# A cached-attention decode kernel: the last V loads in halves released one by one, the keys of pairs 14 and 15 moved up in the load order, and wo in ten pieces

## Chip, cores and metric

One Trainium2 chip; the kernel runs on one of its cores. The metric is device time in microseconds (us). In the profile the engines are PE (TensorE matmuls), PEld (TensorE weight loads), DVE (VectorE), ACT (ScalarE), POOL (GpSimd) and SP (SyncE, which here only issues loads; SPq is its queue). L383 is line 383 of the kernel.

## What is computed

One token goes through a layer norm, then through attention over a cache of 8192 positions in 32 heads, and beside it through a gated unit whose result scales the attention's result. All is float32. Cut to what matters:

```python
xn = layernorm(x)                               # x: 1 x 1 x 512
q  = (xn @ wq)                                  # wq: 512 x 4096, 32 heads of 128
p  = softmax(q . k_cache / sqrt(128))           # k_cache: 32 x 8192 x 128
s  = (p . v_cache) @ wo                         # v_cache the same, wo: 4096 x 512
g  = silu((sigmoid(xn @ w_gate) * (xn @ w_up)) @ w_down)   # 512 x 1376, 1376 x 512
out = x + s * g
```

The two caches are 134.2 MB each, the weights together 25.2 MB; each byte is read once.

## The kernel before, in words

**Tiles.** The 32 heads are taken as NP = 16 pairs. One head of a pair lies on partitions 0 to 63, the other on 64 to 127; each partition holds NB = 128 positions ("columns" below) of 128 numbers, so the keys of a pair, K(i), and its values, V(i), are 8.39 MB each, 64 KB a partition. Three buffers of that size, `slots`, hold them: K of even pairs in slot 1, K of odd pairs in slot 0, every V in slot 2. Pairs are counted from 0, so the last two are 14 and 15.

**One pair.** `scores(i)` (L377) on DVE multiplies the whole of K(i) by the query in place (L383) and sums each position's 128 products (L384), then takes a maximum (L386). PE turns the maximum and spreads it, DVE reduces it (L375, `all_max`), ACT takes the exponentials (L398, `powers_of`) into `weights`. PE then multiplies these by V(i) in 32 matmuls of four columns each (L356, each in two records of the trace, so 64), adding up in `po`. ACT copies `po` (L405), PE gathers the diagonal blocks (L361), DVE places them (L391, `heads_out`). On DVE the order is scores of pair i first, then `heads_out` of pair i - 1, then `all_max` of pair i.

PE's program is noted first and played later: `pair` is one body of a loop over the 16 pairs, so that a wait or count which it contains is there in every pair. All PE instructions therefore carry L37 in the trace. `taken(sem, n)` waits on a semaphore and takes n off it.

**Loads.** All big loads go through SP's one queue in program order, each of them split over the 16 DMA engines. Where an issue has to wait (for a buffer to come free), every load behind it in the program waits too. `summed[i]` counts the end of pair i's scores on DVE and frees its K buffer; `valued` counts pairs whose V matmuls are done and frees slot 2. In the main loop at L408, round i issues K(i) once `summed[i - 2]` is there, then V(i - 1) once `valued` is i - 1. In the last round K(15) and V(14) and V(15) are each cut at column 84 of 128, and the order is K(15) first part, both parts of V(14), K(15) second part, both parts of V(15).

**Output projection.** After V(15), six pieces of wo are issued into slot 1, ending at rows `W_ENDS` = 14, 24, 28, 30, 31, 32 of the 32 rows that a partition holds. Rows below `W_DVE` = 16 are multiplied and added on DVE in two sums, `part` (L466, L468, joined in L472); rows 16 to 29 are matmuls into `big[0]`; `to_fold` adds the two on DVE (L448), and `fold` brings the sum into `acc` by matmuls. Rows 30 and 31 (from `W_FOLD`) go straight into `acc`. Two DVE operations (L497, L499) apply the gate and add x, and SP stores the 2 KB result (L512).

**The start.** Layer norm, the queries and the gated unit run ahead of the loop, while wq, w_gate, w_up and K(0) are loaded; the issues are at the top, ahead of the body.

Of the kernel before, what the change touches and what calls it, by code (L numbers as in the profile page):

```python
# [14 lines left out]
EPS = 1e-5  # L15
# [35 lines left out]
def kernel(  # L51
# [18 lines left out]
    NB = S // HP  # L70
    NP = H // 2
    NG = 4
    GP = P // NG
    GC = D // NG
    QT = 512
    HT = QT // Dh
# [10 lines left out]
    FC = FL // GP  # L87
    assert F <= 3 * QT and FL % GP == 0 and 2 * KT * F <= SLOT and (FP + FC) * D <= SLOT // 2

    W_ENDS, W_DVE, W_FOLD = (14, 24, 28, 30, 31, 32), 16, 30  # L90
    V_CUT, K_CUT = 84, 84

    DVE, ACT, SP, POOL = nc.vector, nc.scalar, nc.sync, nc.gpsimd
    PE = Later(nc.tensor)
# [9 lines left out]
    def sb(name, *shape):  # L104
        return nc.alloc_sbuf_tensor(name, [P, *shape], F32)[:]
# [6 lines left out]
    st, eps_t = sb("st", 16), sb("eps_t", 1)  # L112
    mx, nb, rs, spare = sb("mx", 4), sb("nb", 2), sb("rs", 1), sb("spare", 1)

    pick, half = sb("pick", 2 * HT), sb("half", 2)
    slots = [sb(f"slot{i}", SLOT) for i in range(3)]
    x_row, g_row = sb("x_row", GC), sb("g_row", GC)
    ones, ident = sb("ones", P), sb("ident", P)
# [8 lines left out]
    den = sb("den", H)  # L127
# [14 lines left out]
    def semaphore(name):  # L142
        sems.append(nc.alloc_semaphore(name))
        return sems[-1]
# [11 lines left out]
    pe, dve, act, pool = (Steps(n) for n in ("s_pe", "s_dve", "s_act", "s_pool"))  # L156
    loads = {}

    def load(eng, name, dst, src, *after):
        wait(eng, *after)  # L160
        if name not in loads:
            loads[name] = [semaphore(f"s_{name}"), 0]
        loads[name][1] += 16
        eng.dma_start(dst, src).then_inc(loads[name][0], 16)  # L164
        return loads[name][0], loads[name][1]

    def wait(eng, *steps):
        for s in steps:
            if s is not None:
                eng.wait_ge(*s)  # L170


    turned, spread_m, valued, picked = (semaphore(f"s_{n}") for n in ("turned", "spread", "valued", "picked"))
    maxed, reduced, powers, copied = (semaphore(f"s_{n}") for n in ("maxed", "reduced", "powers", "copied"))
    added = semaphore("s_added")
    s_val = [semaphore(f"s_val{n}") for n in range(2)]


    xv = x.rearrange("a b d -> (a b d)")
# [2 lines left out]
    ld_wq = [load(SP, f"wq{n}", wq_t[:, n:n + 2, :], wq_v[:, n:n + 2, :]) for n in (0, 2)]  # L182
# [7 lines left out]

    ld_k = {}

    FULL, K_LAST, V_LAST = (slice(0, NB),), *((slice(0, c), slice(c, NB)) for c in (K_CUT, V_CUT))

    def cols(j):
        return slice(j.start * Dh, j.stop * Dh)

    def load_keys(i, cut, *after):
        n = (i + 1) % 2
        wait(SP, *after)  # L200
        for j in cut:
            ld_k.setdefault(i, []).append((j, load(SP, f"k{n}_{j.start}", slots[n][:, cols(j)], rows_of(k_cache, i)[:, cols(j)])))

    def load_values(i, cut, *after):

        wait(SP, *after)
        for j, sem in zip(cut, s_val):
            SP.dma_start(slots[2][:, cols(j)], rows_of(v_cache, i)[:, cols(j)]).then_inc(sem, 16)  # L208

    load_keys(0, FULL)  # L210
# [8 lines left out]

    c_xrow = dve(DVE.memset(x_row, 0.0))  # L220
    ld_xr = load(ACT, "xr", x_row[0:P:GP, :], xv.rearrange("(g c) -> g c", g=NG), c_xrow)
    ACT.nop().then_inc(s_val[1], 16 * (NP - 2))
    dve(DVE.memset(ones, 1.0))
    c_eps = dve(DVE.memset(eps_t, EPS))
    c_id = pool(POOL.memset(ident, 0.0))
    wait(POOL, c_id)
    c_id = pool(POOL.affine_select(out=ident, in_=ident, compare_op=ALU.not_equal, fill=1.0, base=0,
                                   pattern=[[-1, P]], channel_multiplier=1))
# [2 lines left out]
    wait(POOL, pool(POOL.memset(half, 0.0)))  # L231
    for e, h in enumerate(HALF):
        c_pool = pool(POOL.memset(half[h, e:e + 1], 1.0))
    wait(DVE, c_id)
    for g in range(NG):
        c_pick = dve(DVE.tensor_copy(pick[g * GP:(g + 1) * GP, :],
                                     ident[g * GP:(g + 1) * GP, g * GP:g * GP + 2 * HT]))


    wait(DVE, ld_xr)  # L240
    x_turned = g_row.rearrange("p (k i) -> p k i", k=KT)
    x_col = x_turned[:, :, 0]
# [1 line left out]
    t = dve(DVE.reduce_sum(st[:, 0:1], x_col, axis=AX.X))  # L244
    wait(PE, t)
    t = pe(PE.matmul(pt[:, 0:1], ones, st[:, 0:1], start=True, stop=True))
    wait(DVE, t)
    t = dve(DVE.tensor_scalar(st[:, 1:2], pt[:, 0:1], 1.0 / D, None, op0=ALU.mult))
    wait(DVE, t)
    t = dve(DVE.tensor_scalar(xc, x_col, st[:, 1:2], None, op0=ALU.subtract))  # L250
    wait(DVE, t)
    t = dve(DVE.tensor_mul(sq, xc, xc))
    wait(DVE, t)
    t = dve(DVE.reduce_sum(st[:, 2:3], sq, axis=AX.X))
    wait(PE, t)
    t = pe(PE.matmul(pm[:, 0:1], ones, st[:, 2:3], start=True, stop=True))
    wait(ACT, t, c_eps)
    t = act(ACT.activation(st[:, 3:4], pm[:, 0:1], AF.Sqrt, bias=eps_t, scale=1.0 / D))
    wait(DVE, t)
    t = dve(DVE.reciprocal(st[:, 4:5], st[:, 3:4]))  # L260
# [10 lines left out]

    wait(DVE, c_xn)
    for k in range(KT - 1):
        wait(DVE, ld_wq[k // 2], t if k else None)
        t = in_place(wq_t, k)
    wait(DVE, t)
    spreads, copies = {}, {}
    for t in range(NQ):
        c = slice(t * QT, (t + 1) * QT)
# [24 lines left out]
    for dst, src, ld in zip(sums, (wg_t, wu_t), (ld_g, ld_u)):  # L304
        wait(DVE, ld)
        for k in range(KT):
            t = in_place(src, k)
            wait(DVE, t)
        wait(PE, t, copies[NQ - 1])
        for d, c in zip(dst, chunks):  # L310
            ins = PE.matmul(d[:, :c.stop - c.start], ones, src[:, 0, c], start=True, stop=True)
# [14 lines left out]
    t = dve(DVE.transpose(hid[:GP, FP:, :], hg[:GP, NG * FW:].rearrange("p (i c) -> p c i", c=FC)))  # L326
    wait(PE, t, ld_d)
    for c in range(FP + FC):
        g, n = c % NG * GP, P if c < FP else GP
        ins = PE.matmul(big[0][g:g + 1, :], hid[:n, c, 0:1], wd_t[:, c, :] if c < FP else wd_last[:, c - FP, :],  # L330
                        start=(c < NG), stop=(c + NG >= FP + FC))
# [8 lines left out]
    def taken(sem, n):  # L340
        PE.wait_ge(sem, n)
        PE.nop().then_inc(sem, -n)

    def pair(v):
        taken(maxed, 1)
        PE.matmul(pt[0:1, :], mx[:, 0:1], ident, start=True, stop=True).then_inc(turned, 1)
        taken(reduced, 1)
        PE.matmul(pm[:, :2], ones[:1, :], mx[:1, 1:3], start=True, stop=True).then_inc(spread_m, 1)
        taken(powers, 2)
        PE.matmul(pm[:GP, 2:], rs.to_broadcast([P, GP]), half, start=True, stop=True).then_inc(added, 1)  # L350

        for j in range(0, NB, HT):
            if j in (0, V_CUT):
                taken(s_val[j > 0], 16)
            g = j // HT % NG
            ins = PE.matmul(po[g * GP:g * GP + 2 * HT, :], weights[:, j // HT, :], v[:, j * Dh:(j + HT) * Dh],  # L356
                            start=(j < HT * NG), stop=(j >= NB - HT * NG))
        ins.then_inc(valued, 1)
        taken(copied, 1)
        for b in range(HT):  # L360
            ins = PE.matmul(pn[:2, :], pick[:, b:2 * HT:HT], o1[:, b * Dh:(b + 1) * Dh],  # L361
                            start=(b == 0), stop=(b == HT - 1))
        ins.then_inc(picked, 1)

    wait(PE, c_pick, c_pool)
    before = PE.take()
    pair(slots[2])
    each = PE.take()


    summed, turned_out = {}, {}
# [36 lines left out]
    for i in range(NP):  # L408
        if i > 0:
            all_max(i - 1)  # L410
        if i >= 2:
            tail = i == NP - 1
            load_keys(i, K_LAST[:1] if tail else FULL, summed[i - 2])
            load_values(i - 1, V_LAST if tail else FULL, (valued, i - 1))
            if tail:
                load_keys(i, K_LAST[1:])
                load_values(i, V_LAST, (valued, i))
        scores(i)
        if i > 0:
            powers_of(i - 1)  # L420
            parts(i - 1)
            heads_out(i - 1)
        if i == 1:
            wait(DVE, c_sig)
            c_gate = dve(DVE.tensor_mul(g_row, g_row, big[1][:, :GC]))
    all_max(NP - 1)
    powers_of(NP - 1)
    wait(DVE, parts(NP - 1))
    t = dve(DVE.reciprocal(den[:GP], den[:GP]))
    heads_out(NP - 1)  # L430
    wait(DVE, t, turned_out[NP - 1])
    heads = o_t[:, :H * WP].rearrange("r (h a) -> r h a", a=WP)
    wait(DVE, dve(DVE.tensor_mul(heads, heads, den[:GP].unsqueeze(2).to_broadcast([GP, H, WP]))))
    for g in range(NG):
# [23 lines left out]
    t_parts = [placed, None]  # L458
    r0 = 0
    for ld, r1 in zip(ld_o, W_ENDS):  # L460
        for r in range(r0, min(r1, W_DVE)):
            n = r % 2
            wait(DVE, ld if r == r0 else None, t_parts[n])
            col = o_all[:, r:r + 1]
            if r < 2:
                ins = DVE.tensor_scalar(part[n], wo_t[:, r, :], col, None, op0=ALU.mult)  # L466
            else:
                ins = DVE.scalar_tensor_tensor(part[n], wo_t[:, r, :], col, part[n], op0=ALU.mult, op1=ALU.add)  # L468
            t_parts[n] = dve(ins)
        r0 = r1  # L470
    wait(DVE, *t_parts)
    t_part = dve(DVE.tensor_add(part[0], part[0], part[1]))  # L472

    wait(PE, placed)
# [1 line left out]
    for ld, r1 in zip(ld_o, W_ENDS):  # L476
# [3 lines left out]
        for r in range(r0, r1):  # L480
            if r < W_FOLD:
                g = r % NG * GP
                ins = PE.matmul(big[0][g:g + 1, :], o_all[:, r:r + 1], wo_t[:, r, :],
                                start=(r < W_DVE + NG), stop=(r + NG >= W_FOLD))
                continue
            for g in range(NG):
                ins = PE.matmul(acc[g * GP:g * GP + 1, :], o_all[:, r:r + 1], wo_t[:, r, g * GC:(g + 1) * GC],
                                start=(r == W_FOLD), stop=(r == WR - 1))
# [4 lines left out]
        if r1 == W_FOLD:  # L493
            parts = to_fold(pe(ins))
        r0 = r1
    wait(DVE, pe(ins), c_gate)
    t = dve(DVE.tensor_mul(g_row, g_row, acc))  # L497
    wait(DVE, t)
    t = dve(DVE.tensor_add(g_row, g_row, x_row))  # L499
# [56 lines left out]
```

## Time and profile before

| | us |
|---|---|
| median of 3 runs | 689.38 |
| lowest and highest | 689.0 and 691.96 |
| the profiled execution's own time | 690.75 |
| its span, first to last instruction | 688.8 |
| DVE busy | 614.6 (89%) |
| PE busy | 215.1 (31%) |
| ACT busy | 42.5 (6%) |

The span is what the trace shows; the profiled execution's own time is 1.95 us longer than it, and the median run is 1.37 us under that time. Starts in the trace are counted from the start of the span. In a row of the timeline the first number is the start, the second the time to the end of the last instruction of the row, and what stands in brackets is the idle time of that engine just before, with what ended it. The granted clock of PE, where a row gives it, is a share of full speed.

### The profile page before, as it was taken

The page shows a single profiled execution, that of the slowest core. Times are in us where ns is not written, and L with a number is a line of the kernel's source. Part 1 is how long each engine was busy: PE and PEld are TensorE (multiplying, and loading weights), DVE is VectorE, ACT ScalarE, POOL GpSimd, SP SyncE. Part 2 cuts the span into 40 slices and gives each one's busy share as a digit, 9 for nine tenths or more (in the row PEclk, how much of TensorE's full clock was granted, in tenths as well). Part 3 has the DMA queues.
Part 4 walks back from the last instruction along what each step waited for, and adds up shares of the span by engine and source line. Part 5 has one row for each costly group of instructions (what it writes and reads, how often), then busy time and mean ns, then how long its engine had stood idle before and what let it go on. Part 6 is the DMA issues. An engine that isn't in the chain of part 4 may idle for free. (4 is left out here: it accounts for less than half of the span.)

```text
span 688.8 us, 3331 instructions
## 1 busy us (share of the span) xinstructions
PE 215.1 (31%) x1366; PEld 62.0 (9%) x1366; DVE 614.6 (89%) x155; ACT 42.5 (6%) x137; POOL 1.2 (0%) x10
## 2 busy tenths in 40 slices
PE   0353024050504315050504214050604124064164
PEld 0120001010100101010100101010101001011010
DVE  4879999999999898998989898998989898999916
ACT  0130010000000101000000101000000101000010
POOL 0000000000000000000000000000000000000000
PEclk9996657575755757575755757575756657576676
DMA  8999999999999999999999999999999999999995
GB/s 373 434 434 453 441 426 426 426 426 426 426 483 430 426 426 426 426 426 453 460 426 426 426 426 426 426 472 441 426 426 426 426 426 426 466 417 426 414 421 231
DMA packets 6688, 293.67 MB, mean 426 GB/s; under 512 B 760, under 2 KB 768, under 8 KB 1184
## 3 DMA queue, kind: packets, MB, share of 16 engines
q1 hardware_dynamic: 6680, 293.67, 98.7%
q10 hardware_dynamic: 8, 0.00, 0.0%
HBM read 293.67 MB, written 0.00 MB: 426 GB/s over the span
## 5 line engine op out<-in xcount | busy, mean ns | idle before, releaser
L383 DVE TENSOR_TENSOR slot<-slot,q_all 128x16384 f32<-128x16384 f32 (+2 forms) x17 | 275.7, 16215 | 27.5 <-DMA slot<-in_A_k_cache_dram 27.5
L384 DVE TENSOR_REDUCE sc<-slot 128x128 f32<-128x16384 f32 (+2 forms) x17 | 275.7, 16216 | 0.6
L37 PE MATMUL po<-slot,weights 128*8 128x512 f32 x1024 | 146.2, 731 | 252.1 <-PEq L37 252.0
L37 PEld LDWEIGHTS po<-slot,weights 128*8 128x8 f32 x1024 | 30.3, 103 | 354.4 <-issue 354.4
L37 PE MATMUL wide<-ident,mx 128*1 128x128 f32 x32 | 9.4, 395 | 120.1 <-PEq L37 120.1
L405 ACT COPY o<-po 128x512 f32<-128x512 f32 x16 | 9.4, 586 | 396.3 <-PE po L37 396.3
L269 DVE SCALAR_TENSOR_TENSOR slot<-slot,xn 128x512 f32<-128x512 f32 (+2 forms) x16 | 24.3, 1552 | 3.0 <-DMA slot<-in_A_wq_dram 2.6
L37 PE MATMUL pn<-o,pick 128*2 128x128 f32 x128 | 16.5, 272 | 12.8 <-PEq L37 12.8
L37 PE MATMUL big<-slot,ones 128*128 128x512 f32 (+1 forms) x28 | 12.6, 600 | 22.3 <-DVE slot L269 20.4
L391 DVE STREAM_TRANSPOSE wide<-pn 32x128 f32<-32x128 f32 x16 | 5.0, 309 | 10.5 <-PE pn L37 10.5
L37 PEld LDWEIGHTS wide<-ident,mx 128*1 128x1 f32 x32 | 1.8, 80 | 124.3 <-issue 124.3
L396 ACT ACTIVATE nb<-pm 128x2 f32<-128x2 f32 x16 | 2.8, 172 | 163.6 <-PE pm L37 163.6
L398 ACT ACTIVATE weights<-sc,nb 64x128 f32<-64x128 f32 x32 | 12.8, 399 | 0.9
L37 PEld LDWEIGHTS pn<-o,pick 128*2 128x2 f32 x128 | 9.9, 84 | 29.6 <-issue 27.2
L375 DVE TENSOR_REDUCE mx<-wide 1x2 f32<-1x128 f32 x16 | 4.5, 279 | 8.7 <-PE wide L37 8.7
L37 PE MATMUL pm<-half,rs 128*32 128x2 f32 x32 | 3.8, 189 | 23.6 <-PEq L37 23.6
L37 PE MATMUL pm<-mx,ones 1*128 1x2 f32 x32 | 8.8, 343 | 7.4 <-PEq L37 7.4
L37 PE MATMUL big<-slot,o 128*1 128x512 f32 (+1 forms) x26 | 5.2, 834 | 13.8 <-DMA slot<-in_B_w_down_dram 13.8
L468 DVE SCALAR_TENSOR_TENSOR q_all<-slot,o_all,q_all 128x512 f32<-128x512 f32 x14 | 9.4, 743 | 0.0
L37 PEld LDWEIGHTS pm<-mx,ones 1*128 1x128 f32 x32 | 7.9, 305 | 14.9 <-issue 14.9
L37 PE MATMUL big<-slot,o_all 128*1 128x512 f32 x28 | 6.5, 1011 | 8.1 <-DMA slot<-in_A_wo_dram 8.1
L285 ACT COPY q_all<-big 64x256 f32<-64x256 f32 x16 | 5.9, 367 | 21.6 <-PE big L37 21.1
(67 smaller groups left out, 58.7 us busy)
## 6 DMA issues: line engine op xcount, KB each, us to landing
slot<-in_A_v_cache_dram SPq DMA_DIRECT2D x2, 5376.0 KB, 16.9
slot<-in_A_wq_dram SPq DMA_DIRECT2D x2, 4096.0 KB, 16.6
slot<-in_A_v_cache_dram SPq DMA_DIRECT2D x2, 2816.0 KB, 23.2
slot<-in_A_k_cache_dram SPq DMA_DIRECT2D x1, 5376.0 KB, 36.1
slot<-in_A_wo_dram SPq DMA_DIRECT2D x1, 3584.0 KB, 31.7
slot<-in_A_k_cache_dram SPq DMA_DIRECT2D x1, 2816.0 KB, 29.0
slot<-in_B_w_gate_dram SPq DMA_DIRECT2D x1, 2752.0 KB, 27.3
slot<-in_B_w_up_dram SPq DMA_DIRECT2D x1, 2752.0 KB, 33.4
```

The source lines that it names most:

```text
L37: ins = getattr(self.engine, name)(*args, **kwargs)
L269: return dve(DVE.scalar_tensor_tensor(y, w[:, k, cols], xn[:, k:k + 1], y, op0=ALU.mult, op1=ALU.add))
L285: copies[t] = act(ACT.copy(qb[h, 2 * t:2 * t + 2, :], q[h, :, e, :]))
L375: DVE.reduce_max(mx[:1, 1:3], pt[0:1, :].rearrange("o (e p) -> o e p", e=2), axis=AX.X).then_inc(reduced, 1)
L383: wait(DVE, dve(DVE.tensor_mul(k[:, j, :], k[:, j, :], qb[:, i:i + 1, :].to_broadcast([P, n, Dh]))))
L384: summed[i] = dve(DVE.reduce_sum(sc[i % 2][:, j], k[:, j, :], axis=AX.X))
L391: turned_out[i] = dve(DVE.transpose(o, pn.rearrange("e (a r) -> e a r", r=WR)))
L396: wait(ACT, act(ACT.mul(nb, pm[:, :2], -SCALE)))
L398: ACT.activation(weights[h, :, e * HT:(e + 1) * HT], sc[i % 2][h].rearrange("p (g b) -> p g b", b=HT), AF.Exp, bias=nb[h, e:e + 1], scale= ...
L405: ACT.copy(o1, po).then_inc(copied, 1)
L468: ins = DVE.scalar_tensor_tensor(part[n], wo_t[:, r, :], col, part[n], op0=ALU.mult, op1=ALU.add)
```

## The change

- V of pairs 12 to 15 is loaded in two pieces, columns 0 to 63 and 64 to 127; the second of pair 15 is cut again at column 104. A new semaphore, `halved`, is counted up by the last matmul of the first half, in every pair. The first piece of V(13), V(14) and V(15) is issued once `halved` says that the first half of the pair before has been used; the others wait for `valued` as before.
- V(12) is no longer issued in round 13 but in round 14, and K(14) is issued in two pieces (cut at column 48) between and behind the halves of V(12). K(15) is issued in two halves, both of them ahead of V(14).
- PE's loop body waits three times for V, at columns 0, 64 and 104, instead of twice. The semaphores of the second and third wait are filled in advance for the pairs whose V comes whole.
- wo comes in ten pieces that end at rows 8, 18, 21, 24, 26, 28, 29, 30, 31, 32, and 18 rows, not 16, are done on DVE.
- At the start, two fills (`ones`, `eps_t`) move from DVE to POOL and four small copies (`pick`) from DVE to ACT; some waits that another wait covers are left out.

The diff, cut to its core:

```diff
-    W_ENDS, W_DVE, W_FOLD = (14, 24, 28, 30, 31, 32), 16, 30
-    V_CUT, K_CUT = 84, 84
+    W_ENDS, W_DVE, W_FOLD = (8, 18, 21, 24, 26, 28, 29, 30, 31, 32), 18, 30
+    V_CUTS, K_HALF, K_FEW = (NB // 2, NB * 13 // 16), NB // 2, NB * 3 // 8
...
-    s_val = [semaphore(f"s_val{n}") for n in range(2)]
+    s_val = [semaphore(f"s_val{n}") for n in range(3)]
+    halved = semaphore("s_halved")
...
+    def pieces(*ends):
+        return [slice(a, b) for a, b in zip((0,) + ends, ends + (NB,))]
+
+    FULL, V_HALVES, V_THREE = pieces(), pieces(V_CUTS[0]), pieces(*V_CUTS)
...
-        for j, sem in zip(cut, s_val):
+        for j in cut:
+            sem = s_val[((0,) + V_CUTS).index(j.start)]
             SP.dma_start(slots[2][:, cols(j)], rows_of(v_cache, i)[:, cols(j)]).then_inc(sem, 16)
...
-    ACT.nop().then_inc(s_val[1], 16 * (NP - 2))
-    dve(DVE.memset(ones, 1.0))
-    c_eps = dve(DVE.memset(eps_t, EPS))
+    ACT.nop().then_inc(s_val[1], 16 * (NP - 4))
+    ACT.nop().then_inc(s_val[2], 16 * (NP - 1))
+    pool(POOL.memset(ones, 1.0))
+    pool(POOL.memset(eps_t, EPS))
...
-    wait(DVE, c_id)
+    wait(ACT, c_pool)
     for g in range(NG):
-        c_pick = dve(DVE.tensor_copy(pick[g * GP:(g + 1) * GP, :],
-                                     ident[g * GP:(g + 1) * GP, g * GP:g * GP + 2 * HT]))
+        act(ACT.copy(pick[g * GP:(g + 1) * GP, :], ident[g * GP:(g + 1) * GP, g * GP:g * GP + 2 * HT]))
...
         for j in range(0, NB, HT):
-            if j in (0, V_CUT):
-                taken(s_val[j > 0], 16)
+            if j in (0,) + V_CUTS:
+                if j == V_CUTS[0]:
+                    ins.then_inc(halved, 1)
+                taken(s_val[((0,) + V_CUTS).index(j)], 16)
...
-        if i >= 2:
-            tail = i == NP - 1
-            load_keys(i, K_LAST[:1] if tail else FULL, summed[i - 2])
-            load_values(i - 1, V_LAST if tail else FULL, (valued, i - 1))
-            if tail:
-                load_keys(i, K_LAST[1:])
-                load_values(i, V_LAST, (valued, i))
+        if 2 <= i < NP - 2:
+            load_keys(i, FULL, summed[i - 2])
+            if i < NP - 3:
+                load_values(i - 1, FULL, (valued, i - 1))
+        elif i == NP - 2:
+
+            few = pieces(K_FEW)
+            load_values(i - 2, V_HALVES[:1], (valued, i - 2))
+            load_keys(i, few[:1], summed[i - 2])
+            load_values(i - 2, V_HALVES[1:])
+            load_keys(i, few[1:])
+            load_values(i - 1, V_HALVES[:1], (halved, i - 1))
+            load_values(i - 1, V_HALVES[1:], (valued, i - 1))
+        elif i == NP - 1:
+            load_keys(i, pieces(K_HALF), summed[i - 2])
+            for v, cut in ((i - 1, V_HALVES), (i, V_THREE)):
+                load_values(v, cut[:1], (halved, v))
+                load_values(v, cut[1:], (valued, v))
```

More of the change, by code (lines that the diff above doesn't have):

```diff
@@ L191 @@
     ld_k = {}
-    FULL, K_LAST, V_LAST = (slice(0, NB),), *((slice(0, c), slice(c, NB)) for c in (K_CUT, V_CUT))
+    def pieces(*ends):
+        return [slice(a, b) for a, b in zip((0,) + ends, ends + (NB,))]
+    FULL, V_HALVES, V_THREE = pieces(), pieces(V_CUTS[0]), pieces(*V_CUTS)
     def cols(j):
@@ L233 @@
         c_pool = pool(POOL.memset(half[h, e:e + 1], 1.0))
-    wait(DVE, c_id)
+    wait(ACT, c_pool)
     for g in range(NG):
-        c_pick = dve(DVE.tensor_copy(pick[g * GP:(g + 1) * GP, :],
-                                     ident[g * GP:(g + 1) * GP, g * GP:g * GP + 2 * HT]))
+        act(ACT.copy(pick[g * GP:(g + 1) * GP, :], ident[g * GP:(g + 1) * GP, g * GP:g * GP + 2 * HT]))
+    wait(DVE, c_pool)
     wait(DVE, ld_xr)
@@ L256 @@
     t = pe(PE.matmul(pm[:, 0:1], ones, st[:, 2:3], start=True, stop=True))
-    wait(ACT, t, c_eps)
+    wait(ACT, t)
     t = act(ACT.activation(st[:, 3:4], pm[:, 0:1], AF.Sqrt, bias=eps_t, scale=1.0 / D))
@@ L273 @@
     for k in range(KT - 1):
-        wait(DVE, ld_wq[k // 2], t if k else None)
+        wait(DVE, ld_wq[k // 2] if k % 2 == 0 else None, t if k else None)
         t = in_place(wq_t, k)
@@ L363, in pair @@
         ins.then_inc(picked, 1)
-    wait(PE, c_pick, c_pool)
     before = PE.take()
@@ L428 @@
     wait(DVE, parts(NP - 1))
-    t = dve(DVE.reciprocal(den[:GP], den[:GP]))
+    dve(DVE.reciprocal(den[:GP], den[:GP]))
     heads_out(NP - 1)
-    wait(DVE, t, turned_out[NP - 1])
+    wait(DVE, turned_out[NP - 1])
     heads = o_t[:, :H * WP].rearrange("r (h a) -> r h a", a=WP)
@@ L470 @@
         r0 = r1
-    wait(DVE, *t_parts)
+    wait(DVE, max(t_parts, key=lambda t: t[1]))
     t_part = dve(DVE.tensor_add(part[0], part[0], part[1]))
@@ L495 @@
         r0 = r1
-    wait(DVE, pe(ins), c_gate)
+    wait(DVE, pe(ins))
     t = dve(DVE.tensor_mul(g_row, g_row, acc))
```

## Prediction, made before the changed kernel was built or run

> **What bounds the kernel now.** I read the page first. The DMA line and the queue table say that one queue moves nearly all the time:
>
> ```profile
> span 688.8 us, 3331 instructions
> ...
> DMA  8999999999999999999999999999999999999995
> ...
> q1 hardware_dynamic: 6680, 293.67, 98.7%
> ```
>
> No edit that moves no byte can shorten the middle. What can be won lies where the queue runs dry, and behind its last byte. So I read the chain of waits, in order of time, from its end:
>
> ```profile
> 640.24 37.24 DMA slot<-in_A_wo_dram
> ...
> 677.61 5.51 PE big L37 x25
> ...
> 684.12 0.70 DVE q_all L448
> ...
> 684.86 0.66 PE wide L37 x16
> ...
> 685.55 0.30 DVE g_row L497
> ...
> 685.87 0.29 DVE g_row L499
> ```
>
> The chain stands on the second wo piece, then on PE. The last DVE operation ends at 686.16, the span 2.64 later. Next the timelines of SP's queue and DVE, for when each load is issued and used:
>
> ```profile
> 573.00 0.33 SPq L208 DMA_DIRECT2D slot<-in_A_v_cache_dram  x1
> 579.57 0.33 SPq L164 DMA_DIRECT2D slot<-in_A_k_cache_dram  x1
> 612.81 0.80 SPq L208 DMA_DIRECT2D slot<-in_A_v_cache_dram  x2
> ...
> 638.91 0.81 SPq L208 DMA_DIRECT2D slot<-in_A_v_cache_dram  x2
> 639.76 3.32 SPq L164 DMA_DIRECT2D slot<-in_A_wo_dram  x6
> ```
>
> ```profile
> 545.07 17.23 DVE L383 TENSOR_TENSOR slot<-slot,q_all 128x16384 f32<-128x16384 f32 x1 [2.74 <-DMA slot<-in_A_k_cache_dram]
> 562.33 17.22 DVE L384 TENSOR_REDUCE sc<-slot 128x128 f32<-128x16384 f32 x1
> ...
> 580.63 0.28 DVE L375 TENSOR_REDUCE mx<-wide 1x2 f32<-1x128 f32 x1 [0.54 <-PE wide L37]
> ...
> 583.74 17.23 DVE L383 TENSOR_TENSOR slot<-slot,q_all 128x16384 f32<-128x16384 f32 x1 [2.83 <-DMA slot<-in_A_k_cache_dram]
> ...
> 618.25 0.29 DVE L386 TENSOR_REDUCE mx<-sc 128x1 f32<-128x128 f32 x1
> ...
> 619.52 11.34 DVE L383 TENSOR_TENSOR slot<-slot,q_all 128x10752 f32<-128x10752 f32 x1
> ...
> 642.66 6.03 DVE L383 TENSOR_TENSOR slot<-slot,q_all 128x5632 f32<-128x5632 f32 x1 [0.42 <-DMA slot<-in_A_k_cache_dram]
> ...
> 654.77 0.29 DVE L386 TENSOR_REDUCE mx<-sc 128x1 f32<-128x128 f32 x1
> ...
> 669.52 0.32 DVE L391 STREAM_TRANSPOSE wide<-pn 32x128 f32<-32x128 f32 x1 [10.52 <-PE pn L37]
> ...
> 671.45 0.88 DVE L466 TENSOR_SCALAR q_all<-slot,o_all 128x512 f32<-128x512 f32 x2 [0.26 <-DMA slot<-in_A_wo_dram]
> 672.25 9.36 DVE L468 SCALAR_TENSOR_TENSOR q_all<-slot,o_all,q_all 128x512 f32<-128x512 f32 x14
> 681.71 0.69 DVE L472 TENSOR_TENSOR q_all<-q_all 128x512 f32<-128x512 f32 x1
> ```
>
> K(13) lands at 545.07 and K(14) at 583.74 (DVE waits for both). Between lie one V and one K, so a load of 8.39 MB takes 38.67 / 2 = 19.33 us. A piece of 84 columns should take 12.69 and one of 44 columns 6.65. Against that I hold the landings, issue plus time to landing (the two 5376 KB rows of V are those issued at 612.81 and 638.91):
>
> ```profile
> slot<-in_A_k_cache_dram SPq DMA_DIRECT2D x1, 5376.0 KB, 36.1
> ...
> slot<-in_A_v_cache_dram SPq DMA_DIRECT2D x1, 5376.0 KB, 16.5
> ...
> slot<-in_A_v_cache_dram SPq DMA_DIRECT2D x1, 5376.0 KB, 17.3
> ...
> slot<-in_A_wo_dram SPq DMA_DIRECT2D x1, 2560.0 KB, 37.2
> ...
> slot<-in_A_wo_dram SPq DMA_DIRECT2D x2, 256.0 KB, 39.8
> ```
>
> K(15)'s first part lands at 579.57 + 36.1 = 615.7. V(14)'s first part lands at 629.3, so 13.6 later instead of 12.69: 0.9 lost, after an issue 2.9 ahead of the landing before it. V(14)'s and K(15)'s second parts end at 642.66, 13.35 later, against 2 x 6.65: nothing lost. V(15)'s first part lands at 656.2, 13.55 later: 0.85 lost, issued 3.75 ahead. In all 1.75 us. The second wo piece lands at 677.5, and the last, issued at about 642.6, at 682.4: 4.9 for 8 of 32 rows, against 4.83 by the rate. So the last byte is there at T = 682.4, and the last DVE operation ends 3.76 later.
>
> **The order of loads, worked out.** From K(13), the halves land every 9.67: V(12) first half 554.7, K(14) first piece (48 columns, 7.25) 562.0, V(12) second half 571.7, K(14) second piece (12.08) 583.7, V(13) 593.4 and 603.1, K(15) 612.7 and 622.4, V(14) 632.1 and 641.75, V(15) 651.4, 657.5 (40 columns) and 661.1 (24 columns).
>
> DVE no longer waits 2.83 for K(14): it can start behind L375, at 580.84, works off the first piece until 593.8, and has the second since 583.7. Scores of pair 14 then end at 615.4 (2 x 17.23 and gaps of 0.1) and those of pair 15, whose keys are both there by 622.4, begin 1.3 later as now and end at 651.3, against 654.75 now: 3.45 earlier (2.83, and 0.42 that L383 waits at 642.66, and 0.2 of start). More pieces cost DVE two more waits, under 0.05 each by the gaps between its rows.
>
> **Is the queue fed?** Each issue hangs on PE's V matmuls:
>
> ```profile
> 564.49 8.45 PE L37 MATMUL po<-slot,weights 128*8 128x512 f32 x64 [19.83 <-PEq L37]
> ...
> 603.16 9.59 PE L37 MATMUL po<-slot,weights 128*8 128x512 f32 x64 [19.92 <-PEq L37]
> ...
> 658.35 9.30 PE L37 MATMUL po<-slot,weights 128*8 128x512 f32 x64
> ...
> 630.21 0.17 PEld L37 LDWEIGHTS po<-slot,weights 128*8 128x8 f32 x4 [0.69 <-issue]
> 631.06 0.17 PEld L37 LDWEIGHTS po<-slot,weights 128*8 128x8 f32 x4 [0.69 <-issue]
> ```
>
> Sixty-four records take 8.45 to 9.59; two matmuls (four weight loads) take 0.85 at the cadence with which each pair begins. Half a V then takes at least 8.45 / 2 = 4.2 and at most 16 x 0.43 = 6.8; I take 5.6, as the slow cadence comes first. V(12) and V(13) have over 15 us to spare. Two places are close. **A:** V(14)'s first half lands at 632.1, `halved` comes at 637.7, and V(15)'s first half is issued 4.05 ahead of 641.75 (2.8 to 5.4 by the bounds). **B:** V(14)'s second half is used at 647.4, and V(15)'s last two pieces with all ten of wo, which stand behind that wait on SP, are issued 4 ahead of 651.4. The loss at each lies between nothing, as for V(13), issued at 573.00, 10.7 ahead, and 1.0, just over the row at 2.9. For B, with many loads issued at once, I take the nearest row, 0.8 (3.75 ahead, eight issues); for A, one load alone, half of it, 0.4. So x = 1.2 in place of 1.75.
>
> **The tail.** The rate gives wo's first piece 4.83 behind V(15), at 665.9, the second at 672.0, and the last row 19.33 behind, at 680.45; ten pieces at the cost of the present last four (0.1) add 0.25. With x, T = 680.7 + 1.2 = 681.9. On the compute side, V(15)'s matmuls begin 3.6 after the scores as now, at 654.9, and take 9.3: 664.2 (columns 104 and up, there by 662.3, are reached at 662.9). L391 follows 1.87 later and L466 1.67 after that: 667.75. Eight rows by 0.40 and 0.669 end at 672.55; the second piece comes at 673.3 with x; ten rows and L472 end at 680.7. On PE, rows 18 to 28 come at 0.60 a row and take 0.44 (5.51 for 25 records, two a row), so PE keeps up. Row 29 lands two rows ahead of T, at 680.65, and with 0.6 for its matmul the sum can be joined at 681.25. That is later than L472, so the load decides. Then L448 0.72, `fold` and row 31 0.70, and L497 with L499 0.63: 683.3, where the present end is 686.16. **Sum: 2.86 us less** (T 0.5 earlier; 2.36 since PE no longer begins 14 rows at 677.61). Two rows more on DVE cost 1.34, inside the 3.45 that the scores give; without that cover they would be in the sum.
>
> **The start**, and PE's added wait and count in each of 16 pairs, I cost at nothing:
>
> ```profile
> 1.78 0.86 DVE L236 COPY pick<-ident 32x8 f32<-32x8 f32 x4
> ...
> 2.67 1.28 ACT L258 ACT_TABLE_LOAD   x1 [2.67 <-DVE pick L236]
> ...
> 10.84 0.26 ACT L258 ACTIVATE st<-pm,eps_t 128x1 f32<-128x1 f32 x1 [6.89 <-PE pm L37]
> ...
> 13.06 2.35 DVE L268 TENSOR_SCALAR slot<-slot,xn 128x4096 f32<-128x4096 f32 x1 [1.50 <-DMA slot<-in_A_wq_dram]
> ```
>
> The four copies (0.86 on DVE) and even a second table load (1.28) fit into ACT's 6.89 of waiting; the chain to L268 has another 1.50 in hand, and beyond that the queue still holds K(0). POOL's two fills stand ahead of what the copies wait for and fall under the same 6.89. PE idles 19.8 in a pair ahead of V (rows above), which hides a count; in the last pair nothing hides it, but the stage at 658.35 takes no longer than the others, with its one such wait.
>
> **Rivals.** All follow from the same sum; the time moves one for one with x.
>
> 1. *The queue is fed in time:* a lead of 4 is enough, x is 0 to 0.6. For it: a piece queued behind another loses nothing (13.35 for two of 44 columns). Against it: 0.85 still lost at 3.75. It gives 685.3 to 685.9.
> 2. *The queue runs dry as now or worse:* PE's halves keep the slow cadence (6.8), so leads fall to 2.9, and the twelve issues of B come late: x is 2 to 4. It gives 687.3 to 689.3.
> 3. *Slower: each boundary of two loads costs what those two showed,* 0.9, whatever the lead. There are eight boundaries more (K(14), V(12), V(13), V(15) one each, wo four): 7.2, and 1.8 at A and B, so x is 9 and the time 694.3. It decides from x = 7.5, or about 0.8 a boundary. Against it: V(14)'s and K(15)'s second parts lost nothing, and wo's last four pieces 0.1. The Trainium skill, DMA: Bandwidth & Descriptors, section Anatomy of one DMA, gives each DMA a fixed cost of about 2.0 us beside its bytes; eight of them would be an estimated 16 us, 702.5 in all. By that rule wo's last four pieces would take about 12.8; the trace, with 4.9, doesn't bear it out for queued loads.
> 4. *The earlier keys give nothing,* because something else holds the scores back: L466 stays at 671.45, 18 rows end with L472 at 683.6, and L472 decides: 685.65 for the last DVE operation, 688.9 in time.
>
> **How the numbers follow.** The sum is made in the profiled execution: 690.75 - 2.86 = 687.9. The median is 1.37 below that execution, so 689.38 - 2.86 = **686.5**. I give the forecast (x from 0.6 to 2, 685.9 to 687.3) 0.40, the first rival 0.32, the second 0.16, the third 0.08, the fourth 0.04. About 0.5% (3.45 us, so 685.93) is what a measurement of this kernel can tell from no change. Faster by more than that: the first rival and the lowest of the forecast's range, 0.36. Slower: the third, 0.08. Within: 0.56. The range runs from 685.0 (x = 0, and 0.3 for the spread of runs, whose lowest is 0.38 under the median) to 689.0 (most of the second rival, and the fourth); the third stays outside.
>
> **What the profile would show.** If I am right: L383 of pair 14 starts at about 580.9 without a wait, the last L386 stands near 651.3, L466 near 667.8, the last wo piece lands at about 682, and the chain's end goes wo, PE, L448, as now, but without five us of PE. A gap between the landing of V(14)'s second half and V(15)'s first half over 10.1 would show a loss at A, one between V(15)'s pieces over 6.3 a loss at B. If L472 ends after PE's row 29, DVE's 18 rows are too many. What makes it wrong: pieces of one or two rows that land over 0.8 apart, V halves that take PE over 7 us, or an L383 of pair 14 or 15 that still waits for its keys.

## The result, and the profile after

The changed kernel takes **687.65 us** (median of 22 runs) against 688.98 us for the kernel before (22 runs). The ratio is 0.9978 with a 95% interval of 0.9972 to 0.9985, so about 1.5 us less (1.3 between the medians). The prediction had 686.5, 2.9 us less, with a range of 685.0 to 689.0. The way was as forecast and the time lies in the range; half of the gain is missing. The execution that was profiled with the result was a slow one (762.78 us, 386 GB/s over the span), so the rows of the changed kernel are those of its second profile, `whole_again` below (688.54 us, span 686.1).

First the timeline of DVE in the changed kernel. Its lines stand for those of before: L389 and L390 for L383 and L384, L392 for L386, L381 for L375, L483, L485 and L489 for L466, L468 and L472, L465 for L448, L516 for L499.

```profile
580.55 0.28 DVE L381 TENSOR_REDUCE mx<-wide 1x2 f32<-1x128 f32 x1 [0.34 <-PE wide L37]
580.75 6.54 DVE L389 TENSOR_TENSOR slot<-slot,q_all 128x6144 f32<-128x6144 f32 x1
...
593.79 10.82 DVE L389 TENSOR_TENSOR slot<-slot,q_all 128x10240 f32<-128x10240 f32 x1
...
616.76 8.67 DVE L389 TENSOR_TENSOR slot<-slot,q_all 128x8192 f32<-128x8192 f32 x1
...
651.51 0.29 DVE L392 TENSOR_REDUCE mx<-sc 128x1 f32<-128x128 f32 x1
...
667.40 0.88 DVE L483 TENSOR_SCALAR q_all<-slot,o_all 128x512 f32<-128x512 f32 x2
...
672.80 6.71 DVE L485 SCALAR_TENSOR_TENSOR q_all<-slot,o_all,q_all 128x512 f32<-128x512 f32 x10 [0.55 <-DMA slot<-in_A_wo_dram]
679.55 0.69 DVE L489 TENSOR_TENSOR q_all<-q_all 128x512 f32<-128x512 f32 x1
681.34 0.69 DVE L465 TENSOR_TENSOR q_all<-q_all,big 128x512 f32<-128x512 f32 x1 [1.10 <-PE big L37]
...
683.09 0.29 DVE L516 TENSOR_TENSOR g_row<-g_row,x_row 128x128 f32<-128x128 f32 x1
```

The reader sees the forecast's times nearly one by one: pair 14's first L389 starts at 580.75 without a wait for its keys (forecast 580.84), the last L392 stands at 651.51 (651.3), L483 at 667.40 (667.75), L489 ends at 680.24 (680.7) and the last operation at 683.38 (683.3). The end of the chain of waits:

```profile
650.54 24.06 DMA slot<-in_A_wo_dram
...
674.74 6.58 PE big L37 x24
...
681.34 0.70 DVE q_all L465
...
682.08 0.66 PE wide L37 x16
```

It is still wo, PE, the join on DVE, `fold`. One sign is not there: the forecast had the chain without five us of PE, and PE still stands in it with 6.58. That PE isn't what holds the end, though: row 29 lands at 680.24 and its matmul ends 1.08 later, and in `warm_6` below, where PE waits for each piece, it ends 1.08 behind its landing too. So the changed kernel is where the sum put it. That the last operation hits the forecast by 0.1 is in part luck: row 29 landed 0.4 earlier than forecast, and its matmul ended 0.5 later behind the landing. What was not where the sum had it is the kernel before. This is its second profile, `before_look` (688.78 us): the page's span, the landings of three loads as in the prediction, SP's timeline, and the tail on DVE.

```profile
span 686.4 us, 3331 instructions
```

```profile
slot<-in_A_k_cache_dram SPq DMA_DIRECT2D x1, 5376.0 KB, 36.1
...
slot<-in_A_v_cache_dram SPq DMA_DIRECT2D x1, 5376.0 KB, 16.2
...
slot<-in_A_wo_dram SPq DMA_DIRECT2D x2, 256.0 KB, 38.8
```

```profile
579.81 0.33 SPq L164 DMA_DIRECT2D slot<-in_A_k_cache_dram  x1
612.44 0.80 SPq L208 DMA_DIRECT2D slot<-in_A_v_cache_dram  x2
...
638.76 0.80 SPq L208 DMA_DIRECT2D slot<-in_A_v_cache_dram  x2
639.60 2.80 SPq L164 DMA_DIRECT2D slot<-in_A_wo_dram  x6
```

```profile
680.92 0.69 DVE L472 TENSOR_TENSOR q_all<-q_all 128x512 f32<-128x512 f32 x1
681.71 0.69 DVE L448 TENSOR_TENSOR q_all<-q_all,big 128x512 f32<-128x512 f32 x1
...
683.47 0.29 DVE L499 TENSOR_TENSOR g_row<-g_row,x_row 128x128 f32<-128x128 f32 x1
```

V(14)'s first part, issued at 612.44, lands 16.2 later, at 628.6. K(15)'s first part landed at 579.81 + 36.1 = 615.9. Between them are 12.7 us, what the rate asks for; in the first profile it was 13.6. V(15)'s first part lands 12.7 behind K(15)'s second part as well (at 654.65, behind 642.00). L448 follows L472 without a wait, so here the sums on DVE hold the end, and neither a load nor PE does. In the first profile the same row has a wait for PE:

```profile
684.12 0.69 DVE L448 TENSOR_TENSOR q_all<-q_all,big 128x512 f32<-128x512 f32 x1 [1.72 <-PE big L37]
```

The span is 2.4 us shorter than in the first profile, and the last operation ends at 683.76 instead of 686.16.

Which of the two is the usual one, the spans of the runs say. Of 91 runs of the kernel before that were taken beside the experiments the median span is 687.0; 79 lie at 687.5 or below, and only 6 reach 688.5. The first profile, with 688.8, is like these few. The changed kernel's median span is 685.7, so the spans differ by 1.3 us.

### The profile page after: what moved, and what is told of

Read it like the earlier page. It is cut to its first block, busy times and chain, and to the rows that moved or that the text cites. A ratio compares the mean times of both kernels' runs of the same rounds, so it can differ in the third digit from the quotient of the medians.

```text
span 760.7 us, 3348 instructions
## 1 busy us (share of the span) xinstructions
PE 218.2 (29%) x1362; PEld 60.2 (8%) x1362; DVE 615.5 (81%) x153; ACT 44.5 (6%) x142; POOL 1.4 (0%) x12
## 5 line engine op out<-in xcount | busy, mean ns | idle before, releaser
L389 DVE TENSOR_TENSOR slot<-slot,q_all 128x16384 f32<-128x16384 f32 (+3 forms) x18 | 275.9, 15325 | 89.1 <-DMA slot<-in_A_k_cache_dram 89.1
L390 DVE TENSOR_REDUCE sc<-slot 128x128 f32<-128x16384 f32 (+3 forms) x18 | 275.8, 15324 | 0.6
L37 PE MATMUL po<-slot,weights 128*8 128x512 f32 x1024 | 154.0, 761 | 384.3 <-PEq L37 384.3
L37 PE MATMUL wide<-ident,mx 128*1 128x128 f32 x32 | 6.7, 294 | 53.2 <-PEq L37 53.2
L485 DVE SCALAR_TENSOR_TENSOR q_all<-slot,o_all,q_all 128x512 f32<-128x512 f32 x16 | 10.8, 747 | 1.8 <-DMA slot<-in_A_wo_dram 1.8
L37 PE MATMUL pm<-mx,ones 1*128 1x2 f32 x32 | 6.9, 281 | 7.4 <-PEq L37 7.4
L381 DVE TENSOR_REDUCE mx<-wide 1x2 f32<-1x128 f32 x16 | 4.4, 275 | 5.1 <-PE wide L37 5.1
L37 PEld LDWEIGHTS pm<-mx,ones 1*128 1x128 f32 x32 | 5.9, 230 | 12.3 <-issue 12.3
L37 PEld LDWEIGHTS big<-slot,ones 128*128 128x128 f32 (+1 forms) x28 | 4.2, 192 | 29.8 <-DVE slot L274 25.4
```

Source lines behind the costliest of these rows:

```text
L37: ins = getattr(self.engine, name)(*args, **kwargs)
L381: DVE.reduce_max(mx[:1, 1:3], pt[0:1, :].rearrange("o (e p) -> o e p", e=2), axis=AX.X).then_inc(reduced, 1)
L389: wait(DVE, dve(DVE.tensor_mul(k[:, j, :], k[:, j, :], qb[:, i:i + 1, :].to_broadcast([P, n, Dh]))))
L390: summed[i] = dve(DVE.reduce_sum(sc[i % 2][:, j], k[:, j, :], axis=AX.X))
```

## The experiments

The first four runs were `whole_again`, `tail_alone`, `order_alone` and `start_alone`, with two theories: Q (the changed kernel's queue loses more than forecast) and R (its tail is longer than forecast). Theory S was formed on their results, before `before_look` was run: the 1.75 us of lost queue time of the first profile belonged to that one execution. "Before" is run beside each; ratios are to it, with 95% intervals. The landings and ends in this table are from each run's own trace:

| run | last wo piece lands | last DVE operation ends | span | ratio to before |
|---|---|---|---|---|
| before, first profile | 682.5 | 686.16 | 688.8 | |
| before_look | 680.9 | 683.76 | 686.4 | |
| start_alone | 680.9 | 684.28 | 687.0 | 0.9998 (0.9986 to 1.0009) |
| tail_alone | 680.9 | 685.64 | 688.3 | 1.0015 (1.0004 to 1.0026) |
| order_alone | 681.1 | 683.23 | 685.9 | 0.9990 (0.9979 to 1.0001) |
| whole_again | 681.6 | 683.38 | 686.1 | 0.9981 (0.9971 to 0.9992) |
| fold_28 | 681.0 | 682.64 | 685.4 | 0.9980 (0.9967 to 0.9992) |
| warm_6 | 681.3 | 683.07 | 685.8 | 0.9986 (0.9978 to 0.9995) |
| pad_56 | 681.1 | 682.95 | 685.7 | 0.9981 (0.9971 to 0.9990) |
| warm_pe | 683.6 | 685.48 | 688.2 | 1.0009 (0.9996 to 1.0022) |
| warm_fold_28 | 683.3 | 684.67 | 687.4 | 1.0004 (0.9996 to 1.0013) |
| warm_6_fold_28 | 682.8 | 684.13 | 686.8 | 1.0011 (1.0002 to 1.0019) |
| no_halved | 690.4 | 692.25 | 695.0 | one run, 697.57 us |

**The changed kernel again.** No edit.

> The changed kernel as it is, for a profile at the usual load rate. The measured gain is about 1.5 us where the prediction had 2.86; this run's trace is to say in which term the rest is. Theory Q (the queue): the last wo piece lands later than 681.9, at about 683.3, because more than 1.2 us is lost at A and B; the stretch from that landing to the last DVE operation is the predicted 1.4. Theory R (the tail): the last wo piece lands at 681.9 as predicted, and the stretch behind it is about 2.8 instead of 1.4, because PE or L472 is late. Time, by both: 1.2 to 1.8 us under the kernel before.

The last piece landed at 681.6 and the last operation ended 1.8 later. Q's 683.3 is out. R's 681.9 is met, but the stretch is 1.8 and not 2.8, so only 0.4 of the missing 1.4 lies there. Neither accounts for it; that led to S.

**The kernel before again.** No edit.

> The kernel before, unchanged, profiled once more. Theory S: the 1.75 us that the first profile lost on the queue (V(14) and V(15) first parts, 0.9 and 0.85) belonged to that one execution, 1.8 us over the median of its kernel, and the term x of the changed kernel was taken off a loss that is not usually there. Then this profile shows V(14)'s first part about 12.7 behind K(15)'s first part, V(15)'s 12.7 behind K(15)'s second, the last wo piece at about 680.9 instead of 682.4, and a span near 687.0. Rival: the loss is the kernel's own at such leads (2.9 and 3.75); then the span is 688.5 or more and the gaps are 13.5.

As S has it: 12.7 behind K(15), 680.9, and 686.4. `start_alone` and `tail_alone`, whose loads up to V(15) are those of before, agree, but they had been run when S was formed: their last wo pieces land at 680.9 too, with V(15) issued at 638.2 and 638.0. So three of four profiles of that load order lose nothing there, and the span of `start_alone`, 687.0, is the median of the runs above.

What was lost in the first profile is in the trace, too. A load counts its semaphore up in 16 steps, and it is there with the last of them. For K(15)'s first part these steps lie within 0.28 us. For V(14)'s first part 15 of them lie within 0.57 and the last comes at 1.17; for V(15)'s first part they are spread over 1.69, and the spread is still 1.74 at the last wo piece. In `before_look` it is 0.25 to 0.34 at all these loads. So it was not the whole queue that ran dry at V(14): one of its 16 streams fell behind, and the later loads came as late. Why it did so in this execution stays open.

**The start edits alone.**

```diff
-    dve(DVE.memset(ones, 1.0))
-    c_eps = dve(DVE.memset(eps_t, EPS))
+    pool(POOL.memset(ones, 1.0))
+    pool(POOL.memset(eps_t, EPS))
...
-        c_pick = dve(DVE.tensor_copy(...))
+        act(ACT.copy(...))
```

> The kernel before with the start edits alone (two fills on POOL, four small copies on ACT, fewer waits). All theories: no difference, within 0.2 us. If it is slower by 0.5 us or more, a part of the missing gain is lost at the start.

No difference, as expected.

**The tail alone, and the order alone.**

```diff
 tail_alone, against before
-    W_ENDS, W_DVE, W_FOLD = (14, 24, 28, 30, 31, 32), 16, 30
+    W_ENDS, W_DVE, W_FOLD = (8, 18, 21, 24, 26, 28, 29, 30, 31, 32), 18, 30
 order_alone, against the changed kernel: the same line, the other way
```

> The kernel before with wo in ten pieces and 18 rows on VectorE, and nothing else. Prediction's sum: DVE starts wo at 671.45 as before, 18 rows and L472 end at 683.6, so DVE decides and the time is 0.5 us less than before. Theory Q agrees (the queue is not touched): 0.3 to 0.7 less. Theory R, if PE with single rows is the late one: no gain, or up to 0.5 us more than before.

> The changed kernel with wo in the old six pieces and 16 rows on VectorE: the new load order, the halves and the start edits alone. Prediction's sum: the last byte lands 0.5 us earlier and PE's 14 rows follow it as before, so 0.5 us less than before. Theory Q: the queue loses about 1.4 us more than I had, so 0.5 to 1.2 us more than before. Theory R: 0.5 us less, as the prediction.

The tail alone is 1.0 us slower than before (0.0015 of 689), which no theory had: the sum had 0.5 less, Q 0.3 to 0.7 less, R at most 0.5 more. DVE in `tail_alone`:

```profile
671.61 10.68 DVE L468 SCALAR_TENSOR_TENSOR q_all<-slot,o_all,q_all 128x512 f32<-128x512 f32 x16
682.39 0.69 DVE L472 TENSOR_TENSOR q_all<-q_all 128x512 f32<-128x512 f32 x1
683.19 0.69 DVE L448 TENSOR_TENSOR q_all<-q_all,big 128x512 f32<-128x512 f32 x1
685.03 0.29 DVE L497 TENSOR_TENSOR g_row<-g_row,wide 128x128 f32<-128x128 f32 x1 [1.16 <-PE wide L37]
```

L472 ends at 683.08, 0.5 ahead of the 683.6 that was expected, and the join follows at once: DVE's 18 rows hold the end. Behind it L497 waits 1.16 for `fold`, where it waited 0.74 in `before_look`: PE's granted clock is 0.50 there against 1.00, after 3.07 us without work against 1.15. The last operation ended at 685.64, where the sum had 685.65 (the two differences cancel, which is luck); but against 683.76 or 684.28 of the usual before that is a loss, and against 686.16 it had looked like a gain. In `order_alone` DVE waits for its first rows, and at the join only 0.24 for PE:

```profile
670.06 0.88 DVE L483 TENSOR_SCALAR q_all<-slot,o_all 128x512 f32<-128x512 f32 x2 [2.94 <-DMA slot<-in_A_wo_dram]
...
680.25 0.69 DVE L489 TENSOR_TENSOR q_all<-q_all 128x512 f32<-128x512 f32 x1
681.19 0.69 DVE L465 TENSOR_TENSOR q_all<-q_all,big 128x512 f32<-128x512 f32 x1 [0.24 <-PE big L37]
```

The heads are ready 2.94 before the big first piece is there. So the new order alone wins about 0.7 (0.999, an interval that just holds 1), the pieces alone lose 1.0, and both together win 1.3: the earlier scores give DVE the time that its two rows more and its smaller first piece then use. The sum and R had 0.5 less for the order alone, but because the last byte would land 0.5 earlier; it lands at 681.1, 0.2 later than in `before_look`, and what came earlier is the last sum of the rows on DVE (L489 ends at 680.94, L472 at 681.61). Q (0.5 to 1.2 slower for the order alone) falls here too.

**What the halves are worth.**

```diff
-                load_values(v, cut[:1], (halved, v))
+                load_values(v, cut[:1], (halved if v < i else valued, v))
```

> The changed kernel with V(15)'s first half waiting for valued (pair 14 done) instead of halved. It shows what the signal from the first half is worth and how long the queue needs from issue to the next landing. By the prediction's model the queue ends with V(14) at 641.9, the issue comes at about 648.5, and the first byte some 2 us later, so V(15)'s first half lands near 660.5 instead of 651.6, 9 us later, and the span is near 694.5 (all of it reaches the end). Rival: the wait is covered, since wo and V(15) are short of compute anyway; then the span grows by 3 us or less.

The rows of `no_halved`, from SP's timeline, the landings and PE's timeline: PE starts on V(14)'s second half at 642.43; V(15)'s first half is issued at 648.77, lands 12.2 later, and PE starts on it at 661.07.

```profile
648.77 1.28 SPq L213 DMA_DIRECT2D slot<-in_A_v_cache_dram  x3
```

```profile
slot<-in_A_v_cache_dram SPq DMA_DIRECT2D x1, 4096.0 KB, 12.2
```

```profile
642.43 6.28 PE L37 MATMUL po<-slot,weights 128*8 128x512 f32 x32 [3.68 <-PEq L37]
...
661.07 5.49 PE L37 MATMUL po<-slot,weights 128*8 128x512 f32 x32 [5.97 <-PEq L37]
```

The span is 695.0, 8.9 more than `whole_again`: the empty queue reaches the end in full, as the model said (9). A half that stands behind another lands 9.67 behind it, so an empty queue costs 12.2 - 9.67 = 2.5 us from the issue on. A lead of about 3 is then on the edge. Nothing was lost at leads of 3.50 and 3.24 in `before_look`, and at 2.90 and 3.72 in `start_alone`; `whole_again` lost 0.4 at 3.2, `order_alone` 0.3 at 3.1, the first profile 0.9 at 2.9 and at 3.7 (there the first of the 16 steps had come 1.2 us ahead of the last, so its lead was 2.6). At 4.1 or more (`fold_28`, `pad_56`) nothing was lost. The Trainium skill, DMA: Bandwidth & Descriptors, gives 0.6 us to the first byte for this path in its Specifications and a fixed cost of about 2.0 us in Anatomy of one DMA (a fit to loads issued by GpSimd, not by SP); the 2.5 measured here on a dry queue is nearer the second.

**Is PE's clock what holds the tail?** One version moves the fold to row 28. Two put matmuls into an unused bank ahead of wo's rows, and two more (`warm_fold_28`, `warm_6_fold_28`) do both.

```diff
 fold_28
-    W_ENDS, W_DVE, W_FOLD = (8, 18, 21, 24, 26, 28, 29, 30, 31, 32), 18, 30
+    W_ENDS, W_DVE, W_FOLD = (8, 18, 21, 24, 26, 28, 29, 30, 31, 32), 18, 28
 warm_pe
+    flat = weights.rearrange("p g b -> p (g b)")
+    for _ in range(14):
+        PE.matmul(big[1][:, :2 * P], ident, flat, start=True, stop=True)
     wait(PE, placed)
 warm_6
     wait(PE, placed)
+    for _ in range(6):
+        PE.matmul(big[1], ident, slots[2][:, :QT], start=True, stop=True)
```

> The changed kernel with W_FOLD 28 instead of 30: rows 28 to 31 go straight into the result as row 30 and 31 did, so that DVE joins the sums after row 27. Theory T1 (PE's lateness behind row 29, 1.1 us instead of the 0.6 of the prediction, is what holds the end): L465 starts 0.9 to 1.1 us earlier and the end follows the last landing, 0.5 to 0.8 us less than the changed kernel, 0.9971 of before. Theory T2 (the two rows more that come in four narrow matmuls each cost PE as much): no difference to the changed kernel, 0.998.

> The changed kernel with 14 matmuls into an unused bank ahead of wo's rows, so that PE does not stand idle for the 9 us before row 18. Theory T1: the granted clock, 0.50 at 672 to 678 in the changed kernel, is 1.0 there; the matmul of row 29 ends 0.5 to 0.7 behind its landing instead of 1.1, and the time is 0.3 to 0.5 us less than the changed kernel (0.9975 of before). Theory T2 (the landing and DVE's sum hold the end, not PE's clock): the clock rises and the time stays, within 0.2 us.

> Both of the two edits above. Theory T1: the join on DVE then follows L489 (680.2), which becomes the limit, and the time is 0.7 to 1.0 us less than the changed kernel, 0.9968 of before. Theory T2: no difference to the changed kernel.

> The changed kernel with 6 wide matmuls (24 instructions, as many more as fold_28 had, which had no early instruction read) into an unused bank right after the heads are placed, to have PE at its full clock when wo's rows come. If no 16 KB read falls into the loop, theory T1: row 29's matmul ends 0.5 to 0.7 us behind its landing instead of 1.1, L465 starts up to 0.5 us earlier, and the time is 0.3 to 0.5 us less than the changed kernel (0.9975 of before). Theory T2: DVE's L489 and the landing hold the end; within 0.2 us of the changed kernel, 0.998.

> The same with W_FOLD 28, the best version that the runs so far point to. Theory T1: the join follows L489 at once (about 679.9 to 680.3), and the time is 0.7 to 1.0 us less than the changed kernel, 0.997 of before. Theory T2: as fold_28, 0.998, since L489 and the four narrow matmuls a row take back what the clock gives.

`warm_6` answers the question of the clock. Two windows of the same stretch, of `whole_again` and of `warm_6` (the number behind POOL's is the granted clock, then the DMA share and GB/s), and behind them PE's timeline in `warm_6`:

```profile
674.00:681.40 7.40, 6.66 (x32) 0.89 (x32) 6.27 (x11) 0.00 (x0) 0.00 (x0) 0.68 0.91 363
```

```profile
674.00:681.40 7.40, 5.57 (x32) 0.74 (x32) 6.29 (x10) 0.00 (x0) 0.00 (x0) 1.00 0.92 369
```

```profile
674.34 1.03 PE L37 MATMUL big<-slot,o_all 128*1 128x512 f32 x6 [1.90 <-DMA slot<-in_A_wo_dram]
676.20 1.03 PE L37 MATMUL big<-slot,o_all 128*1 128x512 f32 x6 [0.83 <-DMA slot<-in_A_wo_dram]
677.50 1.03 PE L37 MATMUL big<-slot,o_all 128*1 128x512 f32 x4 [0.27 <-DMA slot<-in_A_wo_dram]
```

The clock is full, PE waits for each piece, and the time stays (0.9986): T2 for the clock. PE's rows say why: for three rows of wo or for two, a piece's matmuls take 1.03 from their start by the profile, even at the full clock. Row 29's matmul ends 1.08 behind its landing in `whole_again` and in `warm_6` alike: this is the length of a piece's work, not lateness. `fold_28` moves the join forward, from 681.34 to 680.16 (0.55 of it since its last piece lands that much earlier), but the four narrow matmuls of two rows more make the stretch behind it 1.10 instead of 0.66, and the time is that of the changed kernel (0.9980): T2 again. The chain of `fold_28`:

```profile
680.16 0.70 DVE q_all L465
...
680.90 1.10 PE wide L37 x32
```

**A read of the program in the middle of the run.** The three versions with the most matmuls (`warm_pe`, `warm_fold_28`, `warm_6_fold_28`) are slower than the changed kernel (0.9981 in `whole_again`) by 0.0023 to 0.0030 of 689, 1.6 to 2.1 us, which no theory had. The queue table of `warm_pe` for 104 to 112 us has a row that `fold_28` lacks there:

```profile
q8 instruction: 1, 0.02, 0.8%
```

It is one read of 16 KB, at 107.8 in the trace (107.4 in `warm_6_fold_28`); in the others it falls at 685 and later, behind all loads, or is not seen. V(1), issued at 111.34 in `warm_pe` and at 110.72 in `fold_28`, lands 29.8 and 28.7 later, so 1.7 us apart:

```profile
slot<-in_A_v_cache_dram SPq DMA_DIRECT2D x1, 29.8
```

```profile
slot<-in_A_v_cache_dram SPq DMA_DIRECT2D x1, 28.7
```

From the load that lands at 121.4 to 121.9 up to V(14), 15 of the 16 steps in which a load lands are within 0.65 us of one another and the last is 1.3 to 1.4 behind them; from V(15)'s first half on several are late. At the last piece of wo, which lands at 682.8 to 683.6 in these three, the spread is 1.6 to 1.9, against 0.4 to 0.9 in the other versions of the changed kernel. The added matmuls did not make that step late: they run behind 667, more than 500 us later. `pad_56` was to show that the size of PE's program decides where this read falls:

```diff
+    for _ in range(56):
+        PE.nop()
     wait(PE, placed)
```

> The changed kernel with 56 empty PE instructions ahead of wo's rows, where PE waits 9 us anyway: as many as the 14 matmuls of warm_pe come to, without their work. Theory U: in warm_pe a 16 KB instruction read at 107.8 held up one DMA engine for 1.4 us, and as each of the 16 engines is busy without a break, its share of every later load stayed late; the size of PE's program decides whether that read falls there. Then this kernel has the same read near 108, its last wo piece lands 1.4 us after the first engine's more than usual, and it takes 1.0 to 2.0 us more than the changed kernel (ratio to before 1.000 to 1.001). Rival: the loss in warm_pe came of the matmuls (PE at the full clock); then this one is as the changed kernel, 0.998.

It had no such read there and ran as the changed kernel (0.9981). Its rival, that the loss comes of the matmuls at the full clock, had 0.998 for it; but `warm_6` has the full clock and no loss, and the late step is there before any added matmul runs. So the theory of size as I put it failed, or the empty instructions were not in the program at their full size; the trace doesn't list them. What stands is that all three kernels with the early read, and only they, have one late step from 122 us on; that the read makes it late is argued from this. What triggers the read (1374 matmuls in `fold_28` and `warm_6` are without it, 1386 and more have it) stays open, and with it how `warm_6_fold_28` would do without. No version beat the changed kernel clearly.

## Why the prediction was right, and where it was not

- **What bounds the kernel:** right for the changed kernel. The queue is busy to the end, and what empties it reaches the end one for one (`no_halved`: 8.9 us). For the end of the kernel before it holds in the first profile only: in `before_look` and `start_alone` the sums on DVE come last, and the gain comes of the scores that end earlier.
- **The order of loads and DVE:** right within 0.5 us at every step, and no wait for keys in pairs 14 and 15.
- **Is the queue fed:** x was to be 1.2. In `whole_again` V(15)'s first half is issued at 638.77, 3.2 ahead of the landing of V(14)'s second half at 642.0, and lands 13.3 later (the row below) at 652.1, 10.1 behind it instead of 9.67. Again it is one of the 16 steps that is late: the spread goes from 0.48 to 0.88 and stays there. At B the pieces follow at the rate. A half of V took PE 6.3 and 6.5, not 5.6, so the leads were 3.2 and 3.35 instead of 4.05 and 4; that B lost nothing all the same was not foreseen. Taken from the last landings (680.7 + x), x is 0.9 there, of which 0.4 is lost at A, and 0.3 to 0.6 in `fold_28`, `pad_56` and `warm_6`. The taken value came from the rows at 2.9 and 3.75, and these were one execution's.

```profile
slot<-in_A_v_cache_dram SPq DMA_DIRECT2D x1, 4096.0 KB, 13.3
```

- **The tail:** 1.8 behind the last landing instead of 1.4. The 0.6 for row 29's matmul had no row behind it; it is 1.08.
- **The sum of 2.86, and the step to the median:** this is what failed, in the sentences "T 0.5 earlier; 2.36 since PE no longer begins 14 rows at 677.61" and "The median is 1.37 below that execution, so 689.38 - 2.86". Both terms were differences against one execution. In the usual one the queue of before loses nothing, so T comes 0.1 to 0.7 later with the change, not 0.5 earlier. And the stretch from T to the end was 3.76 in the first profile but 2.9 and 3.4 in `before_look` and `start_alone`, where L472 and not PE holds the join (in `before_look` it ends at 681.61, and the join starts at 681.71); against 1.8 in the changed kernel that is about 1.1 to 1.6, not 2.36. Together 0.4 to 1.3 between the profiles, and 1.3 to 1.5 between the runs of both. The 1.37 by which the median lay under the profiled execution was a sign of the same thing: part of what I let the change win, the usual run had already. The sum's end, 683.3, was worked out from the times at which loads land and not from the old end; as a time it gave 687.9, 0.25 from the measured 687.65. Taking 1.37 off it counted the same gain twice. The 689.38 of three runs was besides 0.4 above the median of 22.
- **The rivals:** the third (0.9 a boundary) fell: the eight boundaries more cost at most 0.7 together. The fourth was not so. The measured time lies among those of the second (687.3 to 689.3), and the halves were nearly as slow as it had them, but its x of 2 to 4 is not there: the time came of the base. The first, x of 0.6 or less, is what `order_alone`, `fold_28`, `pad_56` and `warm_6` show and `whole_again` doesn't, but its time, 685.3 to 685.9, shares the wrong base.
- **The cover:** "without that cover they would be in the sum" is what `tail_alone` shows, 1.0 us slower.
- **The start:** nothing, as said.

## What to carry to other kernels

Before a term of under 1% is read from one profile, compare that execution's time with the median: where it lies above by as much as the term, the term may be the execution's own, and it then counts for neither kernel; a second profile of the kernel before would have shown it. In a kernel bound by one load queue, issue each load some 4 us ahead of the end of the one before (at about 3, some executions lost time and some did not), and give a signal from the half-used buffer where a whole one comes too late. Two edits of which each uses what the other frees are to be judged together: here one alone lost 1.0 us and both won 1.3 to 1.5.

## What was not expected of the hardware

- In the three versions with one 16 KB read on the instruction queue in the middle of the saturated run, the load that lands next has one of its 16 steps 1.4 us late. The lateness is not made up before the end, and these versions take 1.6 to 2.1 us more. The same holds for a step that falls behind by 0.4 (`whole_again`) or 0.9 (the first profile).
- A dry queue costs 2.5 us from the issue on (`no_halved`, 12.2 against 9.67), though halves that stand behind one another lose nothing (9.66 to 9.72 apart in `whole_again`).
- SP issued the first eight wo pieces 0.48 us apart and the ninth and tenth about 3 us later each (ten in 9.82 us where six had taken 2.80 to 3.32), still some 22 us ahead of their landing. The row of `whole_again`:

```profile
649.60 9.82 SPq L164 DMA_DIRECT2D slot<-in_A_wo_dram  x10
```
